# Layer-norm scaling of v moved from VectorE to GpSimd, and the copy of the key sums out of PSUM moved from VectorE to ScalarE, in a fused linear-attention and spatial-gating kernel

## The chip, the cores and the metric

The kernel runs on one core of one Trainium2 chip. A core has five engines, each with a queue of its own that is worked off strictly in order: TensorE (PE, matmuls and transposes; PEld are its weight loads), VectorE (DVE), ScalarE (ACT), GpSimd (POOL) and SyncE (SP, here only DMA issue). Engines wait for each other through semaphores. SBUF is the working memory, PSUM the memory that matmuls write to. GpSimd also issues the DMAs that convert fp32 inputs to bf16 on their way in.

The metric is the device time of one execution in microseconds. A change of 2% or more counts as faster or slower.

## What is computed

Two layers in a row, on 8 batches of 576 tokens. The first is attention with a feature map in place of the softmax, over 8 heads of width 64:

```python
def phi(x):
    proj = np.einsum('bhsd,df->bhsf', x, w_phi)
    proj = proj - np.max(np.abs(proj), axis=-1, keepdims=True)
    return np.concatenate([np.exp(proj), np.exp(-proj)], axis=-1)
q_p, k_p = phi(q), phi(k)
kv = np.einsum('bhsf,bhsd->bhfd', k_p, v)
z = np.sum(k_p, axis=2)
num = np.einsum('bhsf,bhfd->bhsd', q_p, kv)
den = np.einsum('bhsf,bhf->bhs', q_p, z)[..., None] + 1e-06
attn = num / den
```

The second is a gated layer that mixes tokens, on x, the 576 x 512 output of a batch's 8 heads side by side:

```python
h = np.maximum(x @ w_in, 0.0)              # 512 -> 1024
u, v = h[..., :512], h[..., 512:]
v_n = (v - mean(v)) / np.sqrt(var(v) + 1e-06)   # over the 512 features
v_s = np.einsum('ts,bsd->btd', w_spatial, v_n) + b_spatial[None, :, None]
out = (u * v_s) @ w_out
```

## The kernel before

A batch's 576 tokens are four blocks of 128 and a tail of 64; the tails of two batches lie side by side in one 128-row unit. The attention works through 36 units: per group of two batches one tail unit and eight pair units, each of two heads of one batch (four pair units make up a batch).

`step(i)` emits one step of a software pipeline. For the newest unit it emits the key part: `a_keys` (matmuls to `ps`, on VectorE the largest absolute value `mk`, on ScalarE the two exponentials `kf`), `a_scale` (ScalarE `em`, then on GpSimd v times `em`, the tile `vs`, two products of 128x512 a unit) and `a_queries` and `a_split` (VectorE `mq`, and its split into two bf16 parts, `mhl`). For the units one to four steps older it emits `a_max_t` (transposed `mhl`, copied by VectorE to `mT`), `a_qfeat` (`pq`, ScalarE `qf`), `a_kv` (40 small matmuls to the PSUM tile `pv`: the sums of key features times v, with their normaliser; they are then copied to the bf16 tile `kv`, line 312), `a_num` (`pn` from `qf` and `kv`; VectorE reciprocal `rc` and product `x`) and `a_x_t` (`x` transposed to `xT`). The `kv` of a unit is made one step before it is read.

When the four pair units of a batch are done, the gated layer of that batch is put into a queue of tasks, and `fill` takes tasks out of it between the parts of the next steps: `b_v_tail` and four `b_v` (matmuls to `pv`, ScalarE relu to `vr`, VectorE statistics `stats` and `mv`), `b_ln` (the normalised `vn`), four `b_u` (ScalarE relu to `uT`), four `b_s` (the spatial matmul, whose weights are `vn` and the tail's `vnt`; VectorE multiplies the result into `uT`), four `b_o` and the tail's part (the output matmul `po`, ScalarE copy to `ob`, DMA out). After the last step the tasks that are left, those of batches 6 and 7, are emitted one after the other with nothing between them. From 300 us on the trace shows only these two batches; that stretch is called the drain below, and the 240 us from 60 to 300, with attention and gated layer mixed, the loop.

In `b_ln` GpSimd makes 1/sqrt(var + 1e-6) in two small instructions (`root`), and VectorE makes `vn` as (vr - mean) * rstd, four instructions of 128x512 in bf16, and one of 64x512 for each batch's tail in `b_v_tail`.

All PSUM tiles, 2 KB a partition each, share one pool of eight. The code gives the order of emission; a list scheduler of the framework then sets the final order on each engine from it, so an edit can shift neighbours on other engines too.

Of the kernel before, what the change touches and what calls it, by code (L numbers as in the profile page):

```python
# [8 lines left out]
FP32 = mybir.dt.float32  # L9
BF16 = mybir.dt.bfloat16  # L10
AF = mybir.ActivationFunctionType
ALU = mybir.AluOpType
# [4 lines left out]
def kernel(  # L17
# [15 lines left out]
    nc = tc.nc  # L33
# [6 lines left out]
    P = 128  # L40
    KC = DM // P
    NP = H // 2
    NB = 4
# [10 lines left out]
    small = ctx.enter_context(tc.tile_pool(name="small", bufs=3))  # L54
# [53 lines left out]
    for i in range(2):  # L108
        r = slice(i * D, (i + 1) * D)
# [20 lines left out]
    def load_weights():  # L130
# [12 lines left out]
                            scalar2=None, op0=ALU.mult)  # L143
    neghalf = cpool.tile([P, NB + 1], FP32)
# [12 lines left out]
    vst, vnt = [], []  # L157
# [140 lines left out]
    def a_kv(u):  # L298
        d, dg, bl = st[u["b"]], gs[u["g"]], u["b"] % 2
        if u["pj"] == 0:  # L300
            d["kv"] = feat.tile([P, H, 2, DA], BF16, tag="kv", name="kv", bufs=3)
        ut = dg["unit"]
        pv = psum.tile([P, 2, 2, DA], FP32, tag="bank", name="pv")
        for hh in range(2):
            h = 2 * u["pj"] + hh
            for s in range(2):
                for c in range(NB):
                    nc.tensor.matmul(out=pv[:, hh, s, :], lhsT=u["kf"][:, s, 4 * hh + c, :],  # L308
                                     rhs=u["vs"][:, s, 4 * hh + c, :], start=(c == 0), stop=False)
                nc.tensor.matmul(out=pv[:, hh, s, :], lhsT=ut["kf"][:, s, h, :],  # L310
                                 rhs=dg["vs"][:, bl, s, h, :], start=False, stop=True)
        nc.vector.tensor_copy(out=d["kv"][:, 2 * u["pj"]:2 * u["pj"] + 2, :, :], in_=pv)  # L312

    def norm(pn, x, r=slice(0, P)):
        n = r.stop - r.start
# [52 lines left out]
    def v_mm(lhs, dst, r, stats, mv):  # L368
        pv = psum.tile([P, HALF], FP32, tag="bank", name="pv")
        for kc in range(KC):  # L370
            nc.tensor.matmul(out=pv[r], lhsT=lhs(kc), rhs=w_in_bf[:, kc, HALF:DFF],  # L371
                             start=(kc == 0), stop=(kc == KC - 1))
        nc.scalar.activation(out=dst[r], in_=pv[r], func=AF.Relu, bias=0.0, scale=1.0)  # L373
        nc.vector.bn_stats(out=stats[r], in_=dst[r])  # L374
        nc.vector.bn_aggr(out=mv[r], in_=stats[r])

    def root(mv, r, n):
        var = small.tile([P, NB, 1], FP32, tag="var", name="var")
        rstd = small.tile([P, NB, 1], FP32, tag="rstd", name="rstd")
        nc.gpsimd.tensor_scalar(out=var[r, 0:n], in0=mv[r, 0:n, 1:2], scalar1=1e-6, scalar2=None, op0=ALU.add)  # L380
        nc.gpsimd.tensor_tensor(out=rstd[r, 0:n], in0=var[r, 0:n], in1=neghalf[r, 0:n].unsqueeze(2), op=ALU.pow)  # L381
        return rstd

    def b_v(b, j):
        d = st[b]
# [9 lines left out]
    def b_ln(b):  # L395
        d = st[b]
        rstd = root(d["mv"], slice(0, P), NB)
        for j in range(NB):
            nc.vector.tensor_scalar(out=d["vn"][:, j, :], in0=d["vr"][j], scalar1=d["mv"][:, j, 0:1],  # L399
                                    scalar2=rstd[:, j, :], op0=ALU.subtract, op1=ALU.mult)  # L400

    def b_v_tail(g, bls):
        d = gs[g]
        r = slice(bls[0] * TL, (bls[-1] + 1) * TL)
        vr = s2.tile([P, HALF], BF16, tag="vr", name="vr", bufs=6)
        stats = small.tile([P, 6], FP32, tag="stats", name="stats")
        mv = small.tile([P, 1, 2], FP32, tag="mv_t", name="mv_t")
        v_mm(lambda kc: d["xTt"][:, kc, r], vr, r, stats, mv[:, 0, :])
        rstd = root(mv, r, 1)
        for bl in bls:  # L410
            r = slice(bl * TL, (bl + 1) * TL)
            nc.vector.tensor_scalar(out=vnt[g % 2][r, bl, :], in0=vr[r], scalar1=mv[r, 0, 0:1],
                                    scalar2=rstd[r, 0, :], op0=ALU.subtract, op1=ALU.mult)

    def b_u(b, dc):
        d = st[b]
# [74 lines left out]
    def unit(i):  # L491
        return units[i] if 0 <= i < NU else None
# [3 lines left out]
    def b_tasks(b):  # L496

        g, bl = b // 2, b % 2
        alone = g in SPLIT
        bls = [bl] if alone else [0, 1]  # L500
        tail = alone or bl == 1
        mm = KC * T0 / 2400.0
        ms = (KC + 1) * T0 / 2400.0
        ts = []
        if tail:
            ts.append((mm, lambda: b_v_tail(g, bls)))
        ts += [(mm, lambda j=j: b_v(b, j)) for j in range(NB)]
        ts.append((0.0, lambda: b_ln(b)))
        ts += [(mm, lambda dc=dc: b_u(b, dc)) for dc in range(KC)]
        if tail:  # L510
            ts.append((mm * len(bls) / 2, lambda: b_u_tail(g, bls)))
            for x in bls:
                ts += [(ms, lambda dc=dc, x=x: b_s(2 * g + x, dc)) for dc in range(KC)]
            ts.append((ms * len(bls) / 2, lambda: b_s_tail(g, bls)))
            for x in bls:
                ts += [(mm, lambda j=j, x=x: b_o(2 * g + x, j)) for j in range(NB)]
            ts.append((mm, lambda: b_o_tail(g, bls)))
        return ts
# [11 lines left out]
    def step(i):  # L530
# [7 lines left out]
        if z and z["pair"]:  # L538
            a_kv(z)
# [32 lines left out]
    for i in range(NU + 4):  # L572
        u = unit(i)
# [47 lines left out]
```

## Time and profile before

| | |
|---|---|
| time, median of 3 runs | 346.89 us (343.25 to 348.12) |
| the profiled execution | 345.98 us |
| its span in the trace | 344.2 us |
| granted TensorE clock, mean | 0.98 |
| instructions on VectorE, ScalarE, GpSimd | 698, 514, 195 |

In the rows of the profile that follow, a group of instructions has its line, its engine, what is written and from what, the shape, and "x" with a count. In rows in order of time the first number is the start in microseconds from the start of the span, the second the time taken; "[1.87 <-POOL rstd L381]" says that the engine was idle for 1.87 us before it, until GpSimd's `rstd` of line 381 was there. Busy times of one engine can overlap a little at the ends, so the distance of two starts is the better price of an instruction in a row of like ones.

### The profile page before, as it was taken

What the parts mean: (1) busy time and instruction counts of PE and PEld (TensorE: products, weight loads), DVE (VectorE), ACT (ScalarE), POOL (GpSimd) and SP (SyncE); (2) the same over time, 40 slices, a digit from 0 to 9 for tenths busy, and PEclk for the clock granted to TensorE, in tenths of its full rate; (3) what the DMA queues carried; (4) which work ended last, traced back from release to release, by engine and by line L of the source; (5) the groups of instructions that cost most, each with busy time, mean ns of one, the idle gap of its engine ahead of it and who ended that gap; (6) DMA issues with size and microseconds to landing.
All of it is one profiled execution on the core that took longest, in us unless ns stands there. A gap on an engine that the chain in (4) does not pass through costs nothing.

```text
span 344.2 us, 8469 instructions
## 1 busy us (share of the span) xinstructions
PE 295.6 (86%) x3370; PEld 199.0 (58%) x3370; DVE 269.9 (78%) x698; ACT 235.1 (68%) x514; POOL 137.4 (40%) x195
## 2 busy tenths in 40 slices
PE   0686688877999889997797999999987999999995
PEld 0365567555676566665554767776554667544442
DVE  6788799686896899788868898879887897385350
ACT  3499377776778786887866856998876664642723
POOL 8399545653243425543713543524333222001010
PEclk9999899998999999999989999999998999999999
DMA  8999995911039205970453009540000000520404
GB/s 111 204 228 210 211 166 76 156 47 31 2 42 273 70 2 67 227 152 2 52 73 124 3 0 161 209 145 11 3 1 2 2 0 5 202 74 0 141 0 137
DMA packets 43773, 31.17 MB, mean 91 GB/s; under 512 B 14355, under 2 KB 38099, under 8 KB 43733
## 3 DMA queue, kind: packets, MB, share of 16 engines
q0 software_dynamic: 27856, 13.77, 29.5%
q1 hardware_dynamic: 15876, 16.85, 16.0%
q8 instruction: 26, 0.43, 0.5%
q14 instruction: 15, 0.11, 0.1%
HBM read 32.85 MB, written 9.44 MB: 123 GB/s over the span
## 4 chain that ended last, share of the span: by engine, by line
DVE 38%; PE 34%; ACT 10%; DMA 7%; POOL 5%; issue 2%; SPq 1%; POOLq 0%; ACTq 0%; DVEq 0%
PE po L463 8%; DVE mk L224 6%; DVE mq L233 5%; ACT kf L227 5%; DVE stats L374 5%; DMA wspt<-in_moe_w_spatial_dram 4%; PE ps L440 4%; DVE x L318 4%; PE pq L282 3%; PE pu L419 3%; DVE uT L443 2%; PE ps L212 2%; POOL rstd L381 2%; DVE vn L399 2%; PE pv L371 2%
## 5 line engine op out<-in xcount | busy, mean ns | idle before, releaser
L244 POOL TENSOR_TENSOR vs<-v_f,em 128x512 bf16<-128x512 f32 x64 | 65.6, 1046 | 99.5 <-ACT em L239 87.9
L227 ACT ACTIVATE kf<-ps 128x512 bf16<-128x512 f32 x144 | 76.1, 623 | 24.6 <-DVE mk L224 24.3
L295 ACT ACTIVATE qf<-pq 128x512 bf16<-128x512 f32 x128 | 66.6, 620 | 31.9 <-PE pq L282 31.7
L224 DVE TENSOR_REDUCE mk<-ps 128x4 f32<-128x512 f32 x72 | 47.2, 674 | 1.6 <-PE ps L212 1.4
L233 DVE TENSOR_REDUCE mq<-ps 128x4 f32<-128x512 f32 x72 | 45.9, 678 | 0.0
L419 PE MATMUL pu<-xT,w_in_bf 128*128 128x512 bf16 x128 | 33.5, 392 | 7.3 <-ACT kf L227 5.2
L465 ACT COPY ob<-po 128x512 f32<-128x512 f32 (+1 forms) x38 | 22.8, 599 | 23.4 <-issue 12.8
L374 DVE BATCH_NORM_STATS2 stats<-vr 128x6 f32<-128x512 bf16 (+1 forms) x38 | 25.6, 681 | 12.4 <-ACT vr L373 12.1
L278 PE MATMUL pq<-qT,wphi 128*128 128x256 bf16 x128 | 32.2, 281 | 3.3 <-DVE kv L312 1.4
L440 PE MATMUL ps<-w_spT,vn 128*128 128x512 bf16 x128 | 33.8, 380 | 1.0 <-DVE vn L399 0.8
L371 PE MATMUL pv<-w_in_bf,xT 128*128 128x512 bf16 x128 | 33.0, 385 | 1.3 <-ACT kf L227 1.3
L282 PE MATMUL pq<-mT,sel 128*128 128x128 bf16 x256 | 28.9, 227 | 5.9 <-DVE mT L268 5.7
L282 PEld LDWEIGHTS <-sel 128*128 128x128 bf16 x256 | 23.5, 101 | 14.6 <-issue 11.9
L463 PE MATMUL po<-w_out_bf,uT 128*128 128x512 bf16 x128 | 31.7, 379 | 0.0
L206 ACT COPY kT<-pt 128x512 bf16<-128x512 bf16 x36 | 21.9, 609 | 10.1 <-PE pt L203 6.3
L373 ACT ACTIVATE vr<-pv 128x512 bf16<-128x512 f32 (+1 forms) x38 | 23.1, 627 | 8.2 <-PE pv L371 7.7
L212 PE MATMUL ps<-wphi,kT 128*128 128x256 bf16 x144 | 24.2, 288 | 4.5 <-ACT kT L206 2.2
L308 PEld LDWEIGHTS <-kf 128*128 128x128 bf16 x512 | 23.5, 98 | 6.2 <-ACT qf L295 0.4
L443 DVE TENSOR_TENSOR uT<-ps,uT 128x512 bf16<-128x512 f32 x32 | 21.8, 682 | 6.3 <-PE ps L441 6.3
L318 DVE TENSOR_TENSOR x<-pn,rc 128x256 bf16<-128x256 f32 x64 | 26.1, 419 | 0.7
L327 PEld LDWEIGHTS <-qf 128*128 128x128 bf16 x512 | 20.2, 97 | 8.3 <-issue 2.6
L419 PEld LDWEIGHTS <-w_in_bf 128*128 128x128 bf16 x128 | 12.6, 100 | 21.5 <-issue 11.3
(108 smaller groups left out, 617.0 us busy)
## 6 DMA issues: line engine op xcount, KB each, us to landing
out_dram<-ob SPq DMA_DIRECT2D x32, 256.0 KB, 2.5
v_f<-in_v_dram SPq DMA_DIRECT2D x6, 1024.0 KB, 6.2
k_bf<-in_k_dram POOLq DMA_DIRECT2D x7, 512.0 KB, 6.0
q_bf<-in_q_dram POOLq DMA_DIRECT2D x7, 512.0 KB, 7.7
v_f<-in_v_dram POOLq DMA_DIRECT2D x2, 1024.0 KB, 8.3
v_tl<-in_v_dram SPq DMA_DIRECT2D x8, 128.0 KB, 4.1
w_in_bf<-in_moe_w_in_dram POOLq DMA_DIRECT2D x1, 1024.0 KB, 12.7
out_dram<-ob SPq DMA_DIRECT2D x8, 128.0 KB, 2.5
```

The lines of the kernel that those rows point to most:

```text
L224: nc.vector.tensor_reduce(out=u["mk"][:, hs], in_=pk, axis=AX.X, op=ALU.max, apply_absolute_value=True)
L227: nc.scalar.activation(out=u["kf"][:, s, hs, :], in_=pk, func=AF.Exp, bias=0.0, scale=sc)
L233: nc.vector.tensor_reduce(out=u["mq"][:, 4 * half:4 * half + 4], in_=pq, axis=AX.X, op=ALU.max, apply_absolute_value=True)
L244: nc.gpsimd.tensor_tensor(out=vs[:, s, :, 0:D], in0=st[u["b"]]["v"][:, pj * H:(pj + 1) * H, :], in1=em[:, s, :].unsqueeze(2).to_broadcast( ...
L282: nc.tensor.matmul(out=pq[:, 2 * par + x, :], lhsT=sel[:, j, :], rhs=m, start=False, stop=(x == 1))
L295: nc.scalar.activation(out=qf[:, s], in_=pq, func=AF.Exp, bias=0.0, scale=sc)
L318: nc.vector.tensor_tensor(out=x, in0=pn[r, :, 0:D], in1=rc[r].to_broadcast([n, 4, D]), op=ALU.mult)
L371: nc.tensor.matmul(out=pv[r], lhsT=lhs(kc), rhs=w_in_bf[:, kc, HALF:DFF], start=(kc == 0), stop=(kc == KC - 1))
L374: nc.vector.bn_stats(out=stats[r], in_=dst[r])
L419: nc.tensor.matmul(out=pu, lhsT=w_in_bf[:, kc, dc * P:(dc + 1) * P], rhs=d["xT"][:, kc, :], start=(kc == 0), stop=(kc == KC - 1))
L440: nc.tensor.matmul(out=ps, lhsT=d["vn"][:, sp, cs], rhs=w_spT[:, sp, 0:T0], start=(sp == 0), stop=False)
L463: nc.tensor.matmul(out=po[r], lhsT=lhs(dc), rhs=w_out_bf[:, dc, :], start=(dc == 0), stop=(dc == KC - 1))
```

## The change

The copy of `pv` to `kv` is issued on ScalarE in place of VectorE. The normalising of v becomes one multiply and add on GpSimd, vr * rstd + (-mean * rstd): `root` now returns both numbers per row and has two more small GpSimd instructions for it, a product of 128x4 (or one column for a tail) and a change of sign. Four large instructions per batch and one per tail leave VectorE, 40 in all, and 40 come to GpSimd; 32 copies go to ScalarE. No DMA is added, removed or issued from another engine.

```diff
-        nc.vector.tensor_copy(out=d["kv"][:, 2 * u["pj"]:2 * u["pj"] + 2, :, :], in_=pv)
+        nc.scalar.copy(out=d["kv"][:, 2 * u["pj"]:2 * u["pj"] + 2, :, :], in_=pv)
...
     def root(mv, r, n):
         var = small.tile([P, NB, 1], FP32, tag="var", name="var")
-        rstd = small.tile([P, NB, 1], FP32, tag="rstd", name="rstd")
+        rs = small.tile([P, NB, 2], FP32, tag="rs", name="rs")
         nc.gpsimd.tensor_scalar(out=var[r, 0:n], in0=mv[r, 0:n, 1:2], scalar1=1e-6, scalar2=None, op0=ALU.add)
-        nc.gpsimd.tensor_tensor(out=rstd[r, 0:n], in0=var[r, 0:n], in1=neghalf[r, 0:n].unsqueeze(2), op=ALU.pow)
-        return rstd
+        nc.gpsimd.tensor_tensor(out=rs[r, 0:n, 0:1], in0=var[r, 0:n], in1=neghalf[r, 0:n].unsqueeze(2), op=ALU.pow)
+        nc.gpsimd.tensor_tensor(out=var[r, 0:n], in0=mv[r, 0:n, 0:1], in1=rs[r, 0:n, 0:1], op=ALU.mult)
+        nc.gpsimd.tensor_scalar(out=rs[r, 0:n, 1:2], in0=var[r, 0:n], scalar1=-1.0, scalar2=None, op0=ALU.mult)
+        return rs
+
+    def normalize(dst, src, rs):
+        nc.gpsimd.tensor_scalar(out=dst, in0=src, scalar1=rs[:, 0:1], scalar2=rs[:, 1:2],
+                                op0=ALU.mult, op1=ALU.add)
...
         for j in range(NB):
-            nc.vector.tensor_scalar(out=d["vn"][:, j, :], in0=d["vr"][j], scalar1=d["mv"][:, j, 0:1],
-                                    scalar2=rstd[:, j, :], op0=ALU.subtract, op1=ALU.mult)
+            normalize(d["vn"][:, j, :], d["vr"][j], rstd[:, j, :])
...
         for bl in bls:
             r = slice(bl * TL, (bl + 1) * TL)
-            nc.vector.tensor_scalar(out=vnt[g % 2][r, bl, :], in0=vr[r], scalar1=mv[r, 0, 0:1],
-                                    scalar2=rstd[r, 0, :], op0=ALU.subtract, op1=ALU.mult)
+            normalize(vnt[g % 2][r, bl, :], vr[r], rstd[r, 0, :])
```

How the instructions move is shown at three places. The first is VectorE at the layer norm of batch 0, before:

```order
L374 BN_STATS stats<-vr 128x6
L337 COPY xT<-pt 128x512
L375 BN_AGGR mv<-stats 128x2
L317 RECIPROCAL rc<-pn 128x4 x2
L318 TENSOR_TENSOR x<-pn,rc 128x4x64
L399 TENSOR_SCALAR vn<-vr,mv,rstd 128x512 x4
L318 TENSOR_TENSOR x<-pn,rc 128x4x64
L224 TENSOR_REDUCE mk<-ps 128x4 x2
L312 CAST kv<-pv 128x264
L233 TENSOR_REDUCE mq<-ps 128x4 x2
```

The same place of VectorE in the changed kernel:

```order
L374 BN_STATS stats<-vr 128x6
L337 COPY xT<-pt 128x512
L375 BN_AGGR mv<-stats 128x2
L317 RECIPROCAL rc<-pn 128x4 x2
L318 TENSOR_TENSOR x<-pn,rc 128x4x64 x2
L224 TENSOR_REDUCE mk<-ps 128x4 x2
L233 TENSOR_REDUCE mq<-ps 128x4 x2
```

The four `vn` and the `kv` between the statistics and the next unit's `mq` are gone; `mk` follows `x` directly.

The second is ScalarE over the same units, before:

```order
L421 ACTIVATE uT<-pu 128x512
L295 ACTIVATE qf<-pq 128x512 x4
L421 ACTIVATE uT<-pu 128x512
L227 ACTIVATE kf<-ps 128x512 x4
L239 ACTIVATE em<-mk 128x8 x2
L421 ACTIVATE uT<-pu 128x512
L206 COPY kT<-pt 128x512
```

And in the changed kernel:

```order
L295 ACTIVATE qf<-pq 128x512 x4
L227 ACTIVATE kf<-ps 128x512 x2
L426 ACTIVATE uT<-pu 128x512
L227 ACTIVATE kf<-ps 128x512 x2
L239 ACTIVATE em<-mk 128x8 x2
L312 CAST kv<-pv 128x264
L426 ACTIVATE uT<-pu 128x512
L206 COPY kT<-pt 128x512
```

The copy to `kv` stands behind the unit's `kf` and `em`, and ahead of the `kT` that the next unit's key matmuls need.

The third is GpSimd in the drain, for the tail and the four blocks of batch 6, before:

```order
L380 TENSOR_SCALAR var<-mv_t 64x1
L381 TENSOR_TENSOR rstd<-var,neghalf 64x1
L380 TENSOR_SCALAR var<-mv 128x4
L381 TENSOR_TENSOR rstd<-var,neghalf 128x4
```

And in the changed kernel:

```order
L381 TENSOR_SCALAR var<-mv_t 64x1
L382 TENSOR_TENSOR rs<-var,neghalf 64x1
L383 TENSOR_TENSOR var<-mv_t,rs 64x1
L384 TENSOR_SCALAR rs<-var 64x1
L388 TENSOR_SCALAR vnt_140<-vr,rs 64x512
L381 TENSOR_SCALAR var<-mv 128x4
L382 TENSOR_TENSOR rs<-var,neghalf 128x4
L383 TENSOR_TENSOR var<-mv,rs 128x4
L384 TENSOR_SCALAR rs<-var 128x4
L388 TENSOR_SCALAR vn<-vr,rs 128x512 x4
```

Two small and four large instructions follow the root on the same queue; no product `vs` is left behind them in the drain. On TensorE the order of the drain's matmuls stays as it was, but for one weight block of `b_v`.

## The prediction

> **What bounds the kernel now.** I read the engine shares, then the busy times by stretch, then the chain of work that ended last, then who waited for whom on TensorE.
>
> ```profile
> PE 295.6 (86%) x3370; PEld 199.0 (58%) x3370; DVE 269.9 (78%) x698; ACT 235.1 (68%) x514; POOL 137.4 (40%) x195
> 60.00:300.00 240.00, 217.37 (x2617) 150.05 (x2615) 199.18 (x521) 177.21 (x393) 92.40 (x129) 0.98 0.35 73
> DVE 38%; PE 34%; ACT 10%; DMA 7%; POOL 5%; issue 2%; SPq 1%; POOLq 0%; ACTq 0%; DVEq 0%
> PE pq L282 <- DVE mT L268: 5.7, 11, 0.9
> PE pu L419 <- ACT kf L227: 5.2, 5, 1.5
> ```
>
> In the loop (second row: PE, PEld, DVE, ACT and POOL busy out of 240 us) TensorE is idle for 22.6 us and VectorE for 41. Neither is full: the chain passes back and forth between them (38% and 34%), and ScalarE has only 10% of it. So relief on VectorE can be worth something, and more work on ScalarE is cheap, but what the loop can gain is limited by TensorE's 22.6 idle microseconds and whatever slow clock goes with them. GpSimd is idle for 60% of the span, mostly waiting for `em`.
>
> **The layer norm in the loop.** At batch 0 the rows in order of time tell the story:
>
> ```profile
> 75.87 0.16 DVE L375 BATCH_NORM_AGGREGATE mv<-stats 128x2 f32<-128x6 f32 x1
> 77.34 1.05 POOL L381 TENSOR_TENSOR rstd<-var,neghalf 128x4 f32<-128x4 f32 x1
> 78.43 1.38 DVE L399 TENSOR_SCALAR vn<-vr,mv,rstd 128x512 bf16<-128x512 bf16 x4 [1.87 <-POOL rstd L381]
> 80.77 2.06 ACT L227 ACTIVATE kf<-ps 128x512 bf16<-128x512 f32 x4 [2.62 <-DVE mk L224]
> 81.91 1.68 PE L419 MATMUL pu<-xT,w_in_bf 128*128 128x512 bf16 x4 [1.50 <-ACT kf L227]
> 123.14 1.02 PE L419 MATMUL pu<-xT,w_in_bf 128*128 128x512 bf16 x4 [1.34 <-ACT kf L227]
> 86.93 1.03 PE L440 MATMUL ps<-w_spT,vn 128*128 128x512 bf16 x4
> ```
>
> VectorE stands 1.87 us for GpSimd's root, then does four `vn`, and only then the next unit's `mk`; `kf` waits for `mk`, and TensorE for `kf`. With `vn` gone from VectorE this whole step goes, here and at the next layer norm (123.14). The other stops of TensorE just behind a layer norm in the loop are these:
>
> ```profile
> 80.19 0.22 PE L267 MATMUL pt<-ident,mhl 128*128 128x128 bf16 x1 [0.84 <-DVE x L318]
> 160.41 1.02 PE L419 MATMUL pu<-xT,w_in_bf 128*128 128x512 bf16 x4 [0.52 <-DVE x L318]
> 186.82 0.38 PE L203 MATMUL pt<-ident,k_bf 128*128 128x128 bf16 x4 [0.35 <-DVE x L318]
> 188.54 1.02 PE L419 MATMUL pu<-xT,w_in_bf 128*128 128x512 bf16 x4 [1.05 <-ACT kf L227]
> 240.75 1.02 PE L419 MATMUL pu<-xT,w_in_bf 128*128 128x512 bf16 x4 [0.20 <-ACT kf L227]
> 262.72 0.27 PE L212 MATMUL ps<-wphi,kT 128*128 128x256 bf16 x1 [1.73 <-DVE qT L207]
> ```
>
> 1.50 + 1.34 + 0.84 + 0.52 + 0.35 + 1.05 + 0.20 + 1.73 = 7.5 us. The four matmuls at 81.91 also took 1.68 us where the same four took 1.02 at 123.14, 0.7 us more right after 2.3 us of idling. **Term 1: -8.2 us** if all of it goes. It could be nothing if the next late thing stops TensorE at the same places (`x`, `mT`); I take it whole, since `mk` comes forward by 3.3 us at batch 0 and no stop is longer than 1.73.
>
> What replaces the wait: `b_s` needs `vn`. At batch 0 it started at 86.93, 10.9 us after the last `mv` (75.87 + 0.16). On GpSimd `vn` will be ready some 5 us after `mv` (below). So the loop hides it, with 5.9 us to spare. Behind the normalising on GpSimd's queue stand `vs` products and input loads; they wait up to 3.5 us longer than now. The `vs` of a unit is read two steps later, and a step lasts about 8 us, so that is hidden too.
>
> **The price on GpSimd** of a multiply-add over 128x512 has no row. The nearest:
>
> ```profile
> L246 POOL CAST vs<-em 128x32 bf16<-128x32 f32 x32 | 6.8, 214 | 5.7 <-ACT em L239 5.7
> 2.36 0.32 POOL masks.py:199 TENSOR_SCALAR_AFFINE_SELECT ident<-ident 128x128 bf16<-128x128 bf16 x1
> L244 POOL TENSOR_TENSOR vs<-v_f,em 128x512 bf16<-128x512 f32 x64 | 65.6, 1046 | 99.5 <-ACT em L239 87.9 <-issue 11.4
> L380 POOL TENSOR_SCALAR var<-mv 128x4 f32<-128x4 f32 x8 | 1.8, 230 | 20.2 <-DVE mv L375 13.2 <-DVE rc L317 6.4 <-DVE mT L268 0.5
> ```
>
> With one tensor read, 96 more columns cost 0.32 - 0.21 = 0.11 us (first two rows), so 512 columns are 0.21 + 480 x 0.0011 = 0.74 us. With two tensors read they are 1.05. I take 0.74, since the new instruction reads one tensor; 0.4 to 1.05 are the ends. The small instructions are like the fourth row, 0.23, and start 0.31 apart.
>
> The Trainium skill (GPSIMD Engine Reference, Performance versus the Vector engine) advises against elementwise work on GpSimd, but gives a loop that reads one input with one or two operations 1.03 cycles an element at 1.2 GHz. By that page 512 columns would be 0.44 us plus the floor, about 0.65 us, an estimate, and the drain's term below 3.7 us instead of 4.4; no run here shows it yet.
>
> **The layer norm in the drain**, where nothing covers it:
>
> ```profile
> 310.21 0.23 POOL L380 TENSOR_SCALAR var<-mv 128x4 f32<-128x4 f32 x1 [5.28 <-DVE mv L375]
> 310.52 1.04 POOL L381 TENSOR_TENSOR rstd<-var,neghalf 128x4 f32<-128x4 f32 x1
> 311.59 1.38 DVE L399 TENSOR_SCALAR vn<-vr,mv,rstd 128x512 bf16<-128x512 bf16 x4 [1.47 <-POOL rstd L381]
> 313.26 0.38 PE L441 MATMUL ps<-w_spT,vnt 128*128 128x512 bf16 x1
> 330.14 1.36 PE L440 MATMUL ps<-w_spT,vn 128*128 128x512 bf16 x4 [0.76 <-DVE vn L399]
> ```
>
> TensorE waits for each `vn` in turn here. The root ends at 311.56; two more small ones at 0.31 put the scales at 312.2; four normalisings put the last `vn` at 312.2 + 4 x 0.74 = 315.2, and the fifth matmul (313.26 now) some 0.3 later, at 315.5. That is +2.2 us for batch 6, and batch 7 repeats it from 328.30 on. **Term 2: +4.4 us** (1.7 at 0.4 us each, 6.9 at 1.05), all of it on the path to the end, since the matmul order there is unchanged.
>
> **The copy of `kv`.**
>
> ```profile
> 81.25 0.42 DVE L312 CAST kv<-pv 128x264 bf16<-128x264 f32 x1
> 81.59 1.28 DVE L233 TENSOR_REDUCE mq<-ps 128x4 f32<-128x512 f32 x2
> L433 ACT ACTIVATE uTt<-pu 128x256 bf16<-128x256 f32 x4 | 1.6, 412 | 0.0
> ```
>
> A copy holds VectorE for 0.34 us (start to start), 32 are 10.9 us, ahead of `mq` and so of `mT`, for which TensorE waits (5.7 us in 11 times, first fence). If it all came off the path the gain would be 10.9, and it is nothing if TensorE only waits for something else. I take some 28 short waits of TensorE for `mT`, `mq`, `qT` and `kv` at 0.16 each: **term 3: -4.5 us**. On ScalarE a copy of 128x256 is 0.41 us; four `kf` take 2.06, so a start-to-start distance is near 0.48 for 512 columns and I estimate 0.27 for 264, 32 x 0.27 = 8.7 us. What covers them is ScalarE's idle time (31.7 us in the span before `qf`); at ScalarE's 10% of the chain they cost **term 4: +0.9 us** (0 to 8.7). The readers of `kv` come one step later.
>
> **VectorE held by GpSimd.** Both split steps of `mhl` take longer while a `vs` runs:
>
> ```profile
> 50.35 2.04 POOL L244 TENSOR_TENSOR vs<-v_f,em 128x512 bf16<-128x512 f32 x2 [4.09 <-ACT em L239]
> 50.84 0.58 DVE L262 CAST mhl<-mq 128x8 bf16<-128x8 f32 x1
> 51.47 0.95 DVE L263 TENSOR_TENSOR mhl<-mq,mhl 128x8 bf16<-128x8 f32 x1
> 62.63 0.15 DVE L262 CAST mhl<-mq 128x8 bf16<-128x8 f32 x1
> L263 DVE TENSOR_TENSOR mhl<-mq,mhl 128x8 bf16<-128x8 f32 x36 | 17.8, 495 | 0.3
> L262 DVE CAST mhl<-mq 128x8 bf16<-128x8 f32 x36 | 17.0, 471 | 0.2
> ```
>
> The cast ends with the first product (51.4), the subtraction with the second (52.4); alone they take 0.15. Each waits for one GpSimd instruction at most. 17.8 + 17.0 - 72 x 0.15 = 24 us of VectorE are lost this way now. The new trains, six in the loop, will catch about one split step each for half to a whole instruction: **term 5: +1.0 us** on the path (0 to 6). This is what the Trainium skill says (SBUF, Who interferes with whom): VectorE and GpSimd share one pair of ports, and whoever is first holds it for the whole instruction; the trace agrees.
>
> **Sum.** 345.98 (the profiled execution: span 344.2 and 1.8 around it) - 8.2 + 4.4 - 4.5 + 0.9 + 1.0 = 339.6 us. That execution is 0.9 under the median of 346.89, so I say 340.0.
>
> **Rivals.**
> - TensorE takes the relief as other waits, and ScalarE's new copies delay `kf` and `kT`: term 3 is 0 and term 4 half of its 8.7, so 345.98 - 8.2 + 4.4 + 4.4 + 1.0 = 347.6. For it: TensorE is already 91% busy in the loop, and the copy stands ahead of `kT` in ScalarE's order. Against: ScalarE's 10% of the chain. Chance 0.20 (344 to 349).
> - The shared port decides: 40 x 0.74 = 30 us more of GpSimd beside the 82 us of large products that now cost 24 us of stalls would bring 24 x 30 / 82 = 8.8 us more, in place of 1.0: 347.4. That is the rule of the Trainium skill (SBUF, Who interferes with whom) taken in full. Against: a train comes once a batch, the split steps once a unit. Chance 0.08.
> - VectorE alone sets the loop: 10.9 for `kv`, about 17 for the loop's `vn`, `vnt` and their waits, 28 in all; two thirds of it in place of terms 1 and 3 give 345.98 - 18.7 + 6.3 = 333.6. For it: 38% of the chain; against: 22.6 us of idle TensorE. Chance 0.17 (328 to 337).
> - The other side: the multiply-add on GpSimd is far dearer than both bounds (the power of 128x4 takes 1.04 us for four columns, so some operations there cost 0.2 us a column). At price t the drain adds 2 x (4t - 0.76). No gain is left from t = 1.85 us; from about 2.2 the loop's `b_s` waits as well (2.0 + 4t is over the 10.9 us) and it is slower by 2%; at 2.5 it is 18.5 for the drain and some 7 in the loop, about 361. Chance 0.10.
>
> **Chances.** My forecast, 336 to 344, gets 0.45. About 2% is what a measurement here can tell from no change, which is 339.95 and 353.8 us; the forecast lies on the lower line, so half of it (0.24) is faster. With the third rival that makes 0.41 faster; 0.21 + 0.20 + 0.08 = 0.49 the same; 0.10 slower. The range 330 to 350 holds the forecast, both rivals near 347 and most of the third.
>
> **What would show it.** Right: `mk` directly behind `x` at each layer norm, TensorE's waits of `pu` for `kf` near 0, `vn` on GpSimd near 0.74 us, the drain 4 us longer from 300 us to the end, `b_s` in the loop never waiting. Wrong: `vn` over 1.1 us, TensorE's idle time in the loop staying near 22 us under other names (ScalarE's `kv` or `kT`), or `mhl` far over 0.5 us on average. A new order of the neighbours by the scheduler, which I haven't priced, could move it by some microseconds either way.

## The result: 5.0% faster, a larger gain than forecast

The changed kernel took 328.42 us (median of 4 runs, 327.36 to 331.39) beside 347.5 us for the kernel before in the same comparison (4 runs, 343.25 to 348.63). The ratio is 0.950, with a 95% interval of 0.940 to 0.959. The forecast was 340.0 us in a range of 330 to 350, so the time lies 1.6 us under the range; the gain is 18 to 19 us where 6.4 were worked out. The profiled execution after took 327.90 us, 18.1 less than the profiled one before.

The page after, its span, the engine shares, the chain that ended last, and the granted clock in 40 slices:

```profile
span 326.1 us, 8471 instructions
PE 284.8 (87%) x3327; PEld 196.4 (60%) x3370; DVE 244.3 (75%) x626; ACT 242.3 (74%) x546; POOL 173.8 (53%) x263
PE 39%; DVE 32%; DMA 11%; ACT 10%; POOL 4%; issue 2%; SPq 1%; POOLq 0%; ACTq 0%; DVEq 0%
PEclk9999899999999999999999999999999999999979
```

VectorE lost 26 us of work and its share of the chain fell from 38% to 32%. ScalarE took over 7 us and kept its 10%. TensorE executes the same work, yet it is busy 11 us less (43 of its matmul records are missing after, which is a small part of it).

The costliest groups that are new or in dispute, after:

```profile
L388 POOL TENSOR_SCALAR vn<-vr,rs 128x512 bf16<-128x512 bf16 x32 | 24.4, 774 | 0.8
L312 ACT CAST kv<-pv 128x264 bf16<-128x264 f32 x32 | 13.5, 421 | 5.6 <-PE pv L310 5.4
L263 DVE TENSOR_TENSOR mhl<-mq,mhl 128x8 bf16<-128x8 f32 x36 | 17.8, 495 | 0.6
L262 DVE CAST mhl<-mq 128x8 bf16<-128x8 f32 x36 | 14.6, 405 | 0.3
```

The split steps `mhl` took 34.8 us before and 32.4 now, so the 30 us of new GpSimd work hold VectorE no longer than the old. In the drain the multiply-add has a clean price, since four stand in a row. Batches 6 and 7 in order of time, after:

```profile
286.93 0.23 POOL L381 TENSOR_SCALAR var<-mv 128x4 f32<-128x4 f32 x1 [3.05 <-DVE mv L375]
289.02 3.04 POOL L388 TENSOR_SCALAR vn<-vr,rs 128x512 bf16<-128x512 bf16 x4
292.34 0.38 PE L446 MATMUL ps<-w_spT,vnt 128*128 128x512 bf16 x1
...
306.66 0.23 POOL L381 TENSOR_SCALAR var<-mv 128x4 f32<-128x4 f32 x1 [0.23 <-DVE mv L375]
308.73 3.04 POOL L388 TENSOR_SCALAR vn<-vr,rs 128x512 bf16<-128x512 bf16 x4
312.22 0.63 PE L446 MATMUL ps<-w_spT,vnt 128*128 128x512 bf16 x1
```

3.04 / 4 = 0.76 us each. From the start of the root to the fifth spatial matmul it is 5.4 us for batch 6 (292.34 - 286.93), where it was 3.05 before (313.26 - 310.21): 2.4 us more, against 2.2 forecast. The last matmul took 0.63 us instead of 0.38: the granted clock had just fallen to half.

### Where the gain came from

The start of ScalarE's `em` marks each of the 36 units, so two kernels can be compared unit by unit, whatever their times. Unit 8 starts its `em` at 62.85 us before and 59.98 after, unit 35 at 283.73 and 261.47. The busy times of the engines between these two marks (stretch; length; PE, PEld, DVE, ACT and POOL busy with their counts; granted clock; DMA share; GB/s), before:

```profile
62.85:283.73 220.88, 199.81 (x2385) 138.21 (x2385) 186.37 (x487) 166.36 (x373) 87.80 (x123) 0.98 0.34 70
```

and after:

```profile
59.98:261.47 201.49, 190.10 (x2351) 135.69 (x2386) 171.38 (x436) 171.38 (x396) 115.62 (x174) 1.00 0.38 78
```

The same 27 steps take 19.4 us less. Of that, 9.7 us are less idle time of TensorE (21.1 to 11.4), and 9.7 stood in the profile of before as busy TensorE. Some of the latter is only missing from the trace (2351 matmul records for 2385), but about half is matmuls at a low clock. The kernel before, in stretches of 2 us around batch 0's layer norm:

```profile
80.00:82.00 2.00, 0.31 (x2) 0.18 (x2) 2.00 (x5) 1.23 (x3) 0.00 (x0) 1.00 0.00 0
82.00:84.00 2.00, 2.00 (x10) 1.06 (x10) 1.08 (x4) 2.00 (x7) 0.99 (x1) 0.53 0.00 0
84.00:86.00 2.00, 2.00 (x34) 2.00 (x32) 1.35 (x3) 1.21 (x3) 1.21 (x3) 0.61 0.00 0
86.00:88.00 2.00, 2.00 (x31) 1.38 (x28) 1.52 (x5) 1.83 (x5) 0.00 (x0) 1.00 0.03 8
```

TensorE stands for 1.7 us, and then the clock is near half for 3.4 us although TensorE is fully busy: (0.47 + 0.39) x 2 = 1.7 us lost by the clock's own account. The same shape stands at 170 and at 262 us, 1.7 us each, 5.1 in all; after has none in this part, and one in the drain. The table gives the three parts of the span for each kernel, with the time lost to low clock in the middle part (one minus the granted clock, over 2 us stretches, added up), and that part without it. What a low stretch really delays can be less than its 1.7 us: e2 and e7 run the same order from unit 13 to unit 35, e7 has one low stretch there and e2 none, and the units keep their distances but for 0.55 us at unit 19 and 1.01 us at unit 22, just behind that stretch. So the figures "at full clock" below are sure to about 0.7 us for each low stretch taken out. The first part has 1.7 to 5.1 us of low clock in every kernel by the same account, and it is not taken out. The experiments are told below.

| kernel | to unit 8 | units 8 to 35 | of it lost to low clock | without it | unit 35 to the end |
|---|---|---|---|---|---|
| before | 62.85 | 220.9 | 5.1 | 215.8 | 60.5 |
| after | 59.98 | 201.5 | 0 | 201.5 | 64.6 |
| e1, `kv` alone | 59.38 | 216.2 | 1.7 | 214.5 | 60.2 |
| e2, layer norm alone | 63.81 | 202.0 | 0 | 202.0 | 63.6 |
| e3, drain on VectorE | 61.28 | 200.8 | 0 | 200.8 | 60.2 |
| e4, `vn` later | 64.22 | 216.2 | 1.7 | 214.5 | 60.4 |
| e5, holds ahead of `mk` | 58.72 | 206.8 | 0 | 206.8 | 64.9 |
| e6, holds behind `mq` | 60.02 | 205.9 | 1.7 | 204.2 | 65.1 |
| e7, `kv` of two batches | 59.03 | 203.3 | 1.7 | 201.6 | 60.5 |
| e8, holds at layer norms | 60.81 | 206.4 | 0 | 206.4 | 64.7 |

For the change this makes: 2.9 us in the first eight units, 14.3 in the middle at full clock, 5.1 less low clock, and 4.2 given back at the end; 2.9 + 14.3 + 5.1 - 4.2 = 18.1 us, the difference of the two profiled executions.

### The profile page after: what moved, and what is told of

It reads as the page before. It is cut to its first block, busy times and chain, and to the rows that moved or that the text cites. A ratio compares the mean times of both kernels' runs of the same rounds, so it can differ in the third digit from the quotient of the medians.

```text
span 326.1 us, 8471 instructions
## 1 busy us (share of the span) xinstructions
PE 284.8 (87%) x3327; PEld 196.4 (60%) x3370; DVE 244.3 (75%) x626; ACT 242.3 (74%) x546; POOL 173.8 (53%) x263
## 4 chain that ended last, share of the span: by engine, by line
PE 39%; DVE 32%; DMA 11%; ACT 10%; POOL 4%; issue 2%; SPq 1%; POOLq 0%; ACTq 0%; DVEq 0%
PE po L468 8%; DVE mq L233 6%; PE ps L445 6%; DVE stats L374 6%; DVE mk L224 5%; DMA wspt<-in_moe_w_spatial_dram 5%; DMA out_dram<-ob 4%; PE ps L212 3%; PE pq L282 3%; ACT qf L295 3%; ACT kf L227 3%; DVE x L318 3%; PE pn L327 3%; PE pu L424 2%; PE pv L308 2%
## 5 line engine op out<-in xcount | busy, mean ns | idle before, releaser
L227 ACT ACTIVATE kf<-ps 128x512 bf16<-128x512 f32 x144 | 77.4, 631 | 11.7 <-DVE mk L224 11.6
L278 PE MATMUL pq<-qT,wphi 128*128 128x256 bf16 x128 | 31.2, 277 | 2.4 <-ACT kf L227 1.8
L424 PE MATMUL pu<-xT,w_in_bf 128*128 128x512 bf16 x120 | 31.6, 379 | 1.4 <-ACT vr L373 0.7
L371 PE MATMUL pv<-w_in_bf,xT 128*128 128x512 bf16 x118 | 31.7, 379 | 1.1 <-ACT kf L227 0.4
L468 PE MATMUL po<-w_out_bf,uT 128*128 128x512 bf16 x118 | 31.0, 379 | 0.5
L206 ACT COPY kT<-pt 128x512 bf16<-128x512 bf16 x36 | 22.6, 628 | 8.4 <-PE pt L203 6.6
L373 ACT ACTIVATE vr<-pv 128x512 bf16<-128x512 f32 (+1 forms) x38 | 24.0, 639 | 6.5 <-PE pv L371 5.8
L327 PE MATMUL pn<-kv,qf 128*128 128x66 bf16 x512 | 22.4, 194 | 3.6 <-ACT kv L312 2.3
L212 PE MATMUL ps<-wphi,kT 128*128 128x256 bf16 x144 | 23.3, 286 | 2.3 <-ACT kT L206 2.3
```

The source lines that it names most:

```text
L227: nc.scalar.activation(out=u["kf"][:, s, hs, :], in_=pk, func=AF.Exp, bias=0.0, scale=sc)
L327: nc.tensor.matmul(out=pn[:, pos, :], lhsT=u["qf"][hh][:, s, pos, :], rhs=d["kv"][:, 2 * u["pj"] + hh, s, :], start=(s == 0), stop=(s == 1))
L424: nc.tensor.matmul(out=pu, lhsT=w_in_bf[:, kc, dc * P:(dc + 1) * P], rhs=d["xT"][:, kc, :], start=(kc == 0), stop=(kc == KC - 1))
L468: nc.tensor.matmul(out=po[r], lhsT=lhs(dc), rhs=w_out_bf[:, dc, :], start=(dc == 0), stop=(dc == KC - 1))
```

## The experiments

Three theories were set against each other. A, position: VectorE's order counts; the wait for the root and four `vn` stand ahead of `mk`, the whole delay is passed on, and the `kv` copies are worth little. B, volume: any microsecond taken off VectorE is worth about 0.8, wherever it stands. C, the forecast's own terms. Nothing of the computation is left out in any of these kernels; the holds of e5, e6 and e8 are extra reductions whose results nobody reads.

### e1 and e2: each half alone

e1 is the kernel before with this line alone, e2 the changed kernel with it undone:

```diff
-        nc.vector.tensor_copy(out=d["kv"][:, 2 * u["pj"]:2 * u["pj"] + 2, :, :], in_=pv)
+        nc.scalar.copy(out=d["kv"][:, 2 * u["pj"]:2 * u["pj"] + 2, :, :], in_=pv)
```

> Only the copy of kv goes to ScalarE; the layer norm stays on VectorE. Theory A (position: VectorE's stop for the layer norm stands directly ahead of the next unit's mk, and the whole stop, wait and four vn, is passed on to the pipeline; the copy of kv does not stand there): little, 341 to 346 us, the units without a layer norm keep their distance. Theory B (volume: any microsecond taken from VectorE in the loop comes back at 0.8): 0.8 x 10.9 = 8.7 less and 0.9 more for ScalarE, about 338 us. Theory C (the terms of the prediction): -4.5 + 0.9, 342.4 us, which this run cannot tell from A.

> Only the layer norm goes to GpSimd; kv stays on VectorE. Theory A: nearly the whole gain, about 331 us (19 us less in the loop, 4.4 us more in the drain). Theory B: 0.8 x 17 = 13.6 less in the loop and 4.4 more in the drain, about 337 us. Theory C: -8.2 + 4.4 + 1.0, about 343 us.

e1 took 337.63 us, a ratio of 0.977 (0.971 to 0.983), so that a gain of 2% is likely and not certain; e2 took 331.12, 0.959 (0.952 to 0.966). e1 speaks for B, e2 for A, and the two gains, 8.6 and 15.1 us under the 346.19 of before, sum to more than both edits together bring. The table resolves it. At full clock e1 gains 1.3 us in the middle part (215.8 to 214.5), although 24 copies have left VectorE there, and 3.5 us in the first eight units; 3.4 us more are low clock, of which e1 has one stretch where before has three. e1 around that stretch:

```profile
78.00:80.00 2.00, 1.28 (x12) 1.11 (x12) 1.91 (x7) 2.00 (x7) 0.33 (x1) 0.66 0.00 0
80.00:82.00 2.00, 2.00 (x31) 2.00 (x30) 0.42 (x1) 2.00 (x6) 1.87 (x3) 0.50 0.01 4
```

Why the copies pay in the first units is seen in one row of before:

```profile
43.75:62.85 19.10, 15.34 (x228) 12.13 (x226) 18.71 (x53) 14.95 (x35) 10.85 (x15) 1.00 0.96 124
```

There VectorE is busy 98% of the time. The DMA engines are busy too (0.96), but e1 does the same three units in 16.6 us with a DMA share of 1.06, so VectorE set the pace. The seven kernels with `kv` on ScalarE reach unit 8 at 58.7 to 61.3 us, the three with it on VectorE at 62.9 to 64.2.

e2 between the same marks:

```profile
63.81:265.77 201.96, 189.97 (x2350) 135.56 (x2385) 176.34 (x457) 165.05 (x372) 114.96 (x173) 1.00 0.37 77
```

It does the 27 steps in 202.0 us, as fast as both edits together (201.5): in this part the layer norm is nearly the whole gain. At full clock it is worth 215.8 - 202.0 = 13.8 us. How much of the 5.1 us of low clock is the layer norm's too isn't settled by these traces: with the layer norm on VectorE they have three, one and one low stretches in this part (before, e1, e4), with it on GpSimd none, none, none and one (after, e2, e3, e7). By groups of TensorE in this part, before (idle time and what ended it last):

```profile
L419 PE MATMUL pu<-xT,w_in_bf 128*128 128x512 bf16 x96 | 26.3, 397 | 7.3 <-ACT kf L227 5.2 <-DVE x L318 0.8 <-ACT uT L421 0.5
L371 PE MATMUL pv<-w_in_bf,xT 128*128 128x512 bf16 x96 | 25.4, 386 | 1.3 <-ACT kf L227 1.3
L212 PE MATMUL ps<-wphi,kT 128*128 128x256 bf16 x108 | 17.1, 274 | 2.3 <-DVE qT L207 2.1 <-ACT uT L421 0.2
```

and in e2:

```profile
L424 PE MATMUL pu<-xT,w_in_bf 128*128 128x512 bf16 x88 | 24.2, 379 | 0.8 <-ACT kf L227 0.2 <-ACT vr L373 0.2
L371 PE MATMUL pv<-w_in_bf,xT 128*128 128x512 bf16 x87 | 24.2, 379 | 0.5
L212 PE MATMUL ps<-wphi,kT 128*128 128x256 bf16 x108 | 16.4, 272 | 0.4 <-DVE qT L207 0.4
```

Idle time ahead of these three groups falls from 10.9 to 1.7 us, and the mean of a 128x512 matmul from 397 and 386 ns to 379. Only a small part comes back under another name: TensorE's longest waits for `mT` in this part, before, in e2, and in e4, which is told below (total, times, longest):

```profile
PE pq L282 <- DVE mT L268: 5.1, 9, 0.9
PE pq L282 <- DVE mT L268: 7.1, 11, 1.5
PE pq L282 <- DVE mT L268: 10.7, 13, 1.8
```

In e2 they grow by 2.0 us while other small stops shrink by as much, so TensorE's idle time falls by 9.1 us in all (21.1 to 12.0).

### e3: the drain's layer norm back on VectorE

```diff
+        pool = b < B - 2
...
+        if pool:
+            nc.gpsimd.tensor_scalar(out=dst, in0=src, scalar1=rs[:, 0:1], scalar2=rs[:, 1:2],
+                                    op0=ALU.mult, op1=ALU.add)
+        else:
+            nc.vector.tensor_scalar(out=dst, in0=src, scalar1=mean, scalar2=rs[:, 0:1],
+                                    op0=ALU.subtract, op1=ALU.mult)
```

> The changed kernel, but the layer norms of batches 6 and 7 and of their tails are made on VectorE as before (subtract and multiply), without the two small GpSimd instructions. All theories have the same drain term: 4.4 us less than the changed kernel, about 324 us, and the stretch from the last batch's first b_v to the end back from 45.3 to 40.9 us. If it stays at 328, the drain was not what the slower GpSimd chain cost.

323.60 us (322.25 to 324.39), ratio 0.935 (0.929 to 0.941): 4.8 us under the changed kernel (in another comparison; against the kernel before in the same comparison the ratios are 0.935 and 0.950), and the best version found. Batch 6's root and `vn` in it:

```profile
288.27 0.23 POOL L380 TENSOR_SCALAR var<-mv 128x4 f32<-128x4 f32 x1 [5.28 <-DVE mv L375]
288.59 1.05 POOL L381 TENSOR_TENSOR rs<-var,neghalf 128x4 f32<-128x4 f32 x1
289.67 1.38 DVE L392 TENSOR_SCALAR vn<-vr,mv,rs 128x512 bf16<-128x512 bf16 x4 [1.49 <-POOL rs L381]
```

The last `vn` is there 2.8 us after the root began, beside 5.1 in the changed kernel. The last part is 60.2 us as before, so the drain's loss is undone whole and nothing in the loop depends on it.

### e4: the same work on VectorE, behind `mk`

```diff
-        ts += [(mm, lambda dc=dc: b_u(b, dc)) for dc in range(KC)]
+        us = [(mm, lambda dc=dc: b_u(b, dc)) for dc in range(KC)]
+        late = 2 if b < B - 2 else 0
+        ts += us[:late] + [(0.0, lambda: b_ln_apply(b))] + us[late:]
```

`b_ln` makes only the root, and `b_ln_apply` issues the four `vn`.

> The kernel before, with the four vn of batches 0 to 5 still on VectorE but issued behind two of the four b_u, so that the root is done when VectorE comes to them, and mk and mq of the next unit stand ahead of them. VectorE does the same work. Theory A: most of the layer norm's gain without any work moved, 332 to 338 us. Theory B: only the 5 us that VectorE stood waiting in the loop come back at 0.8, about 342 us. Theory C: the stops of TensorE behind the layer norm go, -8.2, about 338 us, with no more.

341.83 us, ratio 0.988 (0.981 to 0.995). Batch 0 in order of time shows that the edit did what it should:

```profile
78.84 0.76 DVE L318 TENSOR_TENSOR x<-pn,rc 128x256 bf16<-128x256 f32 x2
79.52 1.28 DVE L224 TENSOR_REDUCE mk<-ps 128x4 f32<-128x512 f32 x2
82.25 0.41 DVE L403 TENSOR_SCALAR vn<-vr,mv,rstd 128x512 bf16<-128x512 bf16 x1
82.56 0.17 DVE L262 CAST mhl<-mq 128x8 bf16<-128x8 f32 x1
82.99 2.09 POOL L244 TENSOR_TENSOR vs<-v_f,em 128x512 bf16<-128x512 f32 x2 [1.89 <-ACT em L239]
83.03 2.20 DVE L403 TENSOR_SCALAR vn<-vr,mv,rstd 128x512 bf16<-128x512 bf16 x2
```

`mk` follows `x` at once and VectorE no longer stands for the root, but the four `vn` now lie between `mq`, `mhl` and `mT`. The gain at the layer norm's unit is lost in the next one (1.89 us gained up to unit 15 and 1.77 lost up to unit 16, for one): 1.3 us remain at full clock, and 3.4 are low clock. The table of waits above shows where it went: TensorE now waits 10.7 us for `mT`, 5.6 more than before. There is a second cost. The last two rows show two `vn` beside two products `vs` of GpSimd; they take 2.20 us, and 1.38 us was the price of four. In the loop the 24 `vn` are busy for 14.0 us in e4 and 9.2 before, so e4 does not leave VectorE's time as it was. B's 342 us was met in total, yet mostly by low clock. So A is wrong in its pure form: `mk` ahead of the layer norm brought next to nothing while the work stayed on VectorE, at this later place. How much of that is `mT`, and how much the collision with `vs`, is not told apart.

### e5, e6 and e8: VectorE held by extra reductions in the changed kernel

```diff
+    HOLD = {12: 1, 17: 2, 25: 4, 28: 6}
...
+            for _ in range(HOLD.get(u["i"], 0) if half == 0 else 0):
+                junk = small.tile([P, 4], FP32, tag="junk", name="junk")
+                nc.vector.tensor_reduce(out=junk, in_=pk, axis=AX.X, op=ALU.max, apply_absolute_value=True)
```

e5 has these 13 reductions (0.60 us each, 7.8 us) ahead of `mk`, e6 has the same ones behind `mq`, at the split. e8 has five each at units 10, 22 and 33, `HOLD = {10: 5, 22: 5, 33: 5}`, ahead of `mk`, where the changed kernel had gained most.

> The changed kernel with VectorE held right ahead of mk in four units that have no layer norm: 1, 2, 4 and 6 extra reductions of the same PSUM tile (0.60 us each: 0.6, 1.2, 2.4, 3.6 us) in units 12, 17, 25 and 28. Read from the start of em, unit by unit, against the changed kernel. Theory A, now with the clock: up to about 0.6 us is swallowed, the longer holds are passed on nearly whole, and where TensorE stops for more than about 1.3 us its granted clock falls to 0.5 for some 3.4 us and 1.7 us more are lost; in all 7.8 us held cost 7 to 11 us, about 336 to 339 us. Theory B: each costs 0.8 of its length, 0.5, 1.0, 1.9, 2.9, in all 6.2 us (334), with the clock unchanged. Theory C (TensorE's named stops are all there is, 0.16 us per short delay): under 4 us in all, below 332.

> The same extra reductions in the same four units, but behind mk and mq, around the two steps of mhl, where the late layer norm of the run before stood. Theory A: less is passed on, since kf can start on time and only mT is late: 3 to 6 us in all, 331 to 334 us, and the clock falls at most at the longest. Theory B: the same 6.2 us as ahead of mk, wherever VectorE is held. Theory C: mT late means TensorE stops, so about as much as ahead of mk.

> Five extra reductions (0.60 us each, 3.0 us of VectorE) ahead of the first mk in units 10, 22 and 33, the units behind a layer norm at which the changed kernel gained most; 9.0 us in all, everything else as in the changed kernel (328.4, loop clock 1.00). If the gain of the layer norm is mk's position at these places, each hold is passed on whole and the low granted clock that the kernel before shows there comes back at two or three of them, 1.7 us each: +9 to +14 us, so 337 to 342, with stretches of granted clock under 0.8 behind the holds. If relief is worth the same anywhere, as the holds at units 12 to 28 were (about 0.7 of what is held, with no fall of the clock): +6, so 334 to 335. If the forecast's listed stops were the whole worth: +3 to +4, so 331 to 333.

One execution each: 332.2, 332.74 and 333.67 us. A's 336 to 339 for e5 is missed, and so are B's 334 and, by little, C's bound of 332; e6 lies in A's range; for e8 the second forecast, 334 to 335, is the nearest, and 337 to 342 is far off. In the middle part at full clock e5 loses 206.8 - 201.5 = 5.3 us of the 7.8 held, e6 2.7 of 7.8 (4.4 with a low stretch that lies behind its third hold), and e8 4.9 of the 8.9 held there. Each hold of e8 first comes through whole (2.99, 3.05 and 2.84 us at its unit), and then 1.15 and 2.14 us of it are made up one unit later behind the first and the third. e8 at unit 33, and its granted clock at units 22 and 33:

```profile
249.22 2.47 DVE L227 TENSOR_REDUCE junk<-ps 128x4 f32<-128x512 f32 x4
251.61 1.27 DVE L228 TENSOR_REDUCE mk<-ps 128x4 f32<-128x512 f32 x2
253.46 0.27 PE L282 MATMUL pq<-qT,wphi 128*128 128x256 bf16 x1 [1.37 <-ACT kf L231]
```

```profile
168.00:170.00 2.00, 0.36 (x2) 0.18 (x2) 2.00 (x5) 1.70 (x4) 0.51 (x1) 1.00 0.00 0
170.00:172.00 2.00, 2.00 (x24) 1.18 (x24) 2.00 (x5) 1.57 (x5) 0.92 (x1) 1.00 0.04 8
252.00:254.00 2.00, 0.58 (x3) 0.29 (x3) 2.00 (x4) 1.94 (x5) 0.16 (x1) 1.00 0.00 0
254.00:256.00 2.00, 2.00 (x31) 1.61 (x31) 1.83 (x9) 1.25 (x5) 1.44 (x2) 1.00 0.00 0
```

TensorE stood for 1.64 us in the first of these stretches, as long as at 80 us in the kernel before, yet the clock stayed at 1.00. The low clock is therefore not a fixed price of a stop of this length, and A's surcharge of 1.7 us per stop is refuted (what decides is shown at the end). Held ahead of `mk`, blocks of 0.6 to 3.6 us cost about half to two thirds of their length here; behind `mq` it is a third, or over half with the low stretch, so that the two places are not told apart by one execution each.

### e7: `kv` on ScalarE for the first two batches alone

On top of e3:

```diff
-        nc.scalar.copy(out=d["kv"][:, 2 * u["pj"]:2 * u["pj"] + 2, :, :], in_=pv)
+        copy = nc.scalar.copy if u["b"] < 2 else nc.vector.tensor_copy
+        copy(out=d["kv"][:, 2 * u["pj"]:2 * u["pj"] + 2, :, :], in_=pv)
```

> The version with the drain's layer norms on VectorE, and kv on ScalarE only for batches 0 and 1, the stretch in which VectorE was busy without a gap; the other 24 copies are back on VectorE. Theory A (relief is worth something only where VectorE is the late engine): no difference to the run with all 32 on ScalarE, 322 to 326 us. Theory B: 24 x 0.34 x 0.8 = 6.5 us more, about 330 us.

324.90 us (324.68 to 325.34), ratio 0.941 (0.935 to 0.948); 1.3 us over e3, which ran on another chip; the two ranges don't touch, but the intervals of the two ratios overlap. 24 copies, 24 x 0.34 = 8.2 us of VectorE, are back, and the middle part is 2.5 us longer, of which 1.7 are one stretch of low clock that e3 didn't have. At full clock they cost 0.8 us (1.5 if the low stretch is taken at the 1.0 us that it delayed). B had 6.5 us and is refuted: spread out in pieces of 0.34 us, the copies fit into VectorE's idle time (201.5 - 171.4 = 30 us between the marks, after).

## Why the forecast was wrong

**The step that failed is term 1**, the layer norm in the loop: -8.2 us forecast, 18.9 measured (e2, unit 8 to 35): 13.8 at full clock, and 5.1 of low clock that went with it in these two traces. Its mechanism was right, and `pu`'s waits for `kf` are gone as it said (5.2 us before, 0.2 in e2). Its size was a sum of single rows of TensorE, picked just behind each layer norm, and even the 13.8 is 1.7 times that. It fell short in three ways.

First, stops were missed. Before, in order of time:

```profile
71.26 1.02 PE L371 MATMUL pv<-w_in_bf,xT 128*128 128x512 bf16 x4 [1.29 <-ACT kf L227]
171.41 1.89 PE L371 MATMUL pv<-w_in_bf,xTt 128*128 128x512 bf16 x4 [0.68 <-DVE xTt L365]
```

The first stands behind the tail's layer norm, which the list didn't look at. A sum over all of TensorE's idle time would have counted them: it falls by 9.1 us, not 7.5, although 2.0 us came back as waits for `mT`, a rival that the term itself named. Second, the low clock was seen at one row (81.91, 1.68 us in place of 1.02) and priced at 0.7 us, the excess of that row alone. It goes on for 3.4 us and stood at three places, 5.1 us. The second row above, 1.89 us, is in one of them. Third, 18.9 - 9.1 - 5.1 = 4.7 us more were busy TensorE at full clock. Some 2 of them are records: e2 lacks 35 matmul records that before has, and e1 and e4, which lack as many, show TensorE 1.9 and 2.5 us less busy at full clock than before. That is a matter of how the gain divides and not of the gain; the rest, some 2.5 us, isn't settled.

The limit named above it, TensorE's 22.6 idle microseconds and the slow clock with them, held: 19.4 us were gained. The term took a third of it. A number much nearer to the gain stood under the same term and was used only to argue that the listed stops would go: `mk` comes forward by 3.3 us at batch 0. From unit 9 to unit 10, just behind it, the changed kernel gained 3.45 us on the kernel before.

**Terms 3 and 4**, the copies, were right in their sum by luck and wrong in their place: -3.6 us forecast. 2.9 us came in the first eight units, where VectorE is full, and 0.5 in the loop. The 28 short waits in the loop that were to pay for it did not: e1 gives 1.3 us there and e7 0.8. The forecast gives no row for the price of 0.16 us each, and no run shows it. ScalarE's price, 0 to 8.7 us, shows as one wait for `kv` itself, in the first units. Who waited for the two moved steps on TensorE, after (total, times, longest):

```profile
PE ps L445 <- POOL vn L388: 4.5, 5, 1.1
PE pn L327 <- ACT kv L312: 2.3, 1, 2.3
```

The second is that one. The first lies in the drain with all its five times, so `b_s` in the loop never waits for the normalising, as forecast.

**Term 2**, the drain, had the mechanism right and a size that low clock helped to meet: +4.4 forecast, 64.66 - 60.48 = 4.2 measured, in which one stretch of low clock lies (1.7); e2, without such a stretch, has 3.2, and e3 wins 4.8 by undoing it. The price of the multiply-add, 0.74 us forecast, is 0.76. The Trainium skill's rate (GPSIMD Engine Reference, Performance versus the Vector engine) had given an estimate of 0.65 us; the trace has it 0.11 dearer. The same section also has about 1.8 cycles an element as a best case, 769 ns measured for 512 elements, and the trace agrees with that figure.

**Term 5**, VectorE held by GpSimd, +1.0 forecast, is nil: `mhl` took 32.4 us in place of 34.8. The rival of the shared port falls with it.

**The rivals.** TensorE took back only 2.0 us as other waits, and the multiply-add was not dear. (The price at which a dear one would have left no gain is 1.54 us by the forecast's own terms, 2 x (4 x 1.54 - 0.76) = 10.8, and not 1.85.) The third rival, that VectorE sets the loop, at 333.6 us and a chance of 0.17, was the nearest. It came near in total, by luck, and not in kind: it had two thirds of 28 us of VectorE work, wherever it stands. The layer norm gave 0.8 of its 17 us at full clock, the copies in the loop 0.8 to 1.3 us of some 8. Its chance of 0.17, and 0.41 in all for faster, were too low: the wait of 1.87 us and the four `vn` in front of `mk`, in the forecast's own rows, spoke for it.

What stays open: why the layer norm passes on 0.8 of its length and a hold of the same length 0.5 to 0.7; half of the 4.7 us; what e4 loses to `vs` and what to `mT`; and how much of the low clock is the layer norm's.

## What to carry to other kernels

Price relief on an engine by stretch and by the size of the piece. Here a block of microseconds that stood ahead of the next unit's first step, with a wait for another engine in it, came back at 0.8 of its length; small copies spread over a loop in which the engine has idle time came back at a tenth to a fifth, and paid only where it was full. Sum idle time over a whole stretch and not by rows picked out, and look for stretches in which a busy TensorE runs at a low clock. Move an operation to a slower engine only where something covers it: the loop gained 14 us by it at full clock, the drain lost 3 to 4, and e3, which moves the one and not the other, beats both kernels.

## What was not expected of the hardware

Short stops of TensorE, 1.2 to 1.7 us within 2 us, can be followed by 3.4 us at half clock, which takes away up to 1.7 us, and the number of such stretches differs from execution to execution. The Trainium skill (TensorE: Matmul & The Clock Gate, HAM oscillation) has the clock fall after gaps of more than about 3.4 us; here shorter gaps were enough at 80, 170 and 262 us, and equal ones in e8 were not.

The traces show what tells them apart. In each of the ten, all changes of the granted clock lie on one grid with a pitch of 3.41 us, whose place differs from trace to trace, and each low stretch is one or two whole cells of that grid. Count the columns of the matmuls that begin in a cell (512 for a 128x512 one) in the 886 cells at full clock; half of the cells between 64 and 280 us have 7,200 or more. All 18 cells with fewer than 2,500 columns were followed by half clock, 12 of the 22 with 2,500 to 3,200, and none of the 846 with more. The kernel before had 2,176, 2,560 and 2,336 in the cells ahead of its three stretches; e8's stop at 168 us lies in a cell with 3,022. So a stop of the same length is harmless or not by how it falls on the grid and how little else the cell holds. Between 2,500 and 3,200 the count alone doesn't decide.

The kernel before shows the effect on whole times, seven executions on one chip (mean granted clock, and time):

| clock | 0.990 | 0.980 | 0.980 | 0.975 | 0.975 | 0.972 | 0.970 |
|---|---|---|---|---|---|---|---|
| us | 342.82 | 345.19 | 345.54 | 346.36 | 346.96 | 346.19 | 347.61 |

So 0.02 of mean clock goes with 4.8 us, and most of the spread of the kernel before on this chip is this. On a second chip the two executions with the highest clock, 0.985, are again the shortest (343.04 and 343.26 us), but the other five, 0.970 to 0.980, lie without order at 345.78 to 347.34. The changed kernel's four executions have 0.977 to 0.987, and its slowest, 331.39 us, the lowest of these. Without any low clock from unit 8 on, 5.1 us before and 1.7 in the drain after, the profiled pair would differ by about 14.7 us instead of 18.1.

On GpSimd a multiply-add of two numbers per row over 128x512 in bf16 costs 0.76 us, while VectorE does the like at 1.38 / 4 = 0.35 us.
